# One more buffer for the rows of q and k, and three copies of v moved up on their queue

## The chip, the core and the metric

The kernel runs on one NeuronCore of a Trainium2 chip. The metric is the device time of one execution in microseconds (us), as the median over several runs. The profile is that of a single execution. Its engines are called PE (matrix multiply; PEld is the loading of its weights), DVE, ACT and POOL (element work), and SP, which here only issues DMAs and passes signals on. POOL issues DMAs of its own as well.

## What is computed

A layer normalisation of x (2048 tokens by 448), then two branches: attention with 16 heads of 28 over eight keys per query, two positions apart, and a feed-forward of width 1792. The two are multiplied and added to x.

```python
xn = _layernorm(x, axis=-1)
# A: q, k, v = xn @ wqkv; each query sees positions pos - 2*[0..7]
logits = einsum("bhsd,bhswd->bhsw", q, kg) * Dh ** -0.5     # masked below position 0
s = (softmax(logits) @ vg) @ wo
# B
g = silu(gelu(xn @ w1 + b1) @ w2 + b2)
return x + s * g
```

## The kernel before

**Tiles.** The tokens are put into 16 tiles of 128 (t = 0 to 15), even positions first, so that a dilation of two becomes neighbours. Four tiles make a chunk. The attention works on nine blocks of queries that do not coincide with the tiles: a block needs scores (L595, PE), exponentials (L605, ACT), a mask (L611, DVE or POOL), and the product with the values (L627, PE). The last step of all is the product with wo (L681), the gate and the sum.

**The order is written out.** Every piece of work is a task with a number, and the string ORDER (L17) lists all of them, with a letter for the engine that does each: P for PE, V for DVE, A for ACT, G for POOL, S for SP, D for the landing of a DMA. Each engine goes through its own tasks in this order and stops at the first one whose inputs are not there, with all behind it.

**The rows of q and k.** For a tile, PE makes q and k with tokens on partitions (L454, in `pair`, two outputs side by side in two banks). ACT and DVE copy each bank into a buffer of that tile in SBUF (`evac` of `qk_rows`, L456 to L464, the copies by the helper at L228 on ACT and L230 on DVE). Such a copy also frees its bank for PE. When both are done, SP issues one DMA that transposes the buffer into `qkT` (L276), where the scores read it. There are four such buffers, `qk_tok[t % 4]`, so the copies of tile t wait until the transpose of tile t - 4 has landed (`t_qk.get(t - len(qk_tok))`, L461). Their padding columns are zeroed once at the start, by one memset on DVE each (L255).

In the first two chunks the transposes are issued in the order t = 0, 2, 1, 3, with four transposes of `xn` between 2 and 1. The copies out of the banks for the second chunk stand in the order 6, 5, 4, 7 on ACT and on DVE. PE finishes the tiles of the second chunk in the order 6, 7, 5, 4. Behind the copies of tile 7, ACT has the first layer's activations (`ff1`, L516) and PE the matmuls that feed them (L512); these take the banks that the copies free, two for each pair of 512-column outputs.

**The copies of v.** v stays with tokens on partitions, in `v_tok[t]` (copied out of the banks by L228 and L230). A block's values must lie in windows of 64 rows that cross the tiles, so POOL issues DMAs that copy pieces of `v_tok` into one of six buffers `v` (`values` at L485, the DMA at L270). A copy whose piece belongs to a buffer that another copy has opened takes the same buffer. Tasks 407, 399, 403 and 405 copy rows of tile 8; 409, 411 and 415 copy rows of tile 9. Tasks 399, 403 and 405 fill the last rows of the buffers v2 and v3, which the fifth block's values read (the block in the middle, 56 queries wide). Tasks 409, 411 and 415 fill parts of v4 and v5 for the block after that. On POOL they stood as 407, 409, 411, 415, 399, 403, 405.

Every DMA of SP and of POOL raises one of eight semaphores in turn, and waits until the eighth DMA before it on its queue has landed.

Of the kernel before, what the change touches and what calls it, by code (L numbers as in the profile page):

```python
# [11 lines left out]
ACT = mybir.ActivationFunctionType  # L12
# [28 lines left out]
V744 P463 A464 A465 P468 S466 D467 G450 P451 V453 P442 G469 V751 P470 A471 V739 P435 S443 P444 V740 A446 A445 A566  # L41
G436 P437 A439 V753 V472 P754 V438 S440 D441 P868 P763 V452 V759 A766 V760 V869 P873 V870 V761 V567 V874 A768 A770
V762 A764 S447 D448 P578 P579 V580 A576 V577 V755 P781 A786 P373 A782 A788 V756 S871 D872 S861 D862 P583 S584 G374
P375 V376 G407 D408 P585 A784 A56 A377 P588 A581 S589 V757 G409 D410 V758 G411 D412 V767 V765 P593 P392 S594 A587
P590 P595 A586 G415 D416 V769 G399 D400 V771 V875 S393 A591 G403 D404 G473 P603 S876 D877 P394 S604 A597 P608 V395
A596 G405 D406 G413 D414 G417 D418 V789 G474 D475 P605 V787 A396 P772 G476 D477 G478 D479 G480 D481 A592 G482 D483
A606 V785 G484 D485 G486 D487 P598 V582 A607 S609 V773 V774 G488 D489 P613 V775 G490 D491 V783 S599 P600 G492 D493
V776 G494 D495 A602 A601 S614 P615 A616 P610 V777 V778 V779 V780 A612 P790 V795 P618 V791 A617 V796 A611 A57 P799
A800 V797 V798 G496 D497 P888 V889 P619 V620 P878 A804 V890 P883 A802 G498 D499 P817 S891 D892 V879 A818 V803 G500
# [69 lines left out]
def kernel(  # L119
# [13 lines left out]
    P = 128  # L133
    S, D, H, DH, F = A_x.shape[1], 448, 16, 28, 1792
# [16 lines left out]
    for v in range(9):  # L151
        n = NW - 1 if v == 4 else NW
        q = 4 * NW * v - 4 * (v > 4)
# [17 lines left out]
    def sb(name, shape, dt=BF16):  # L171
        return const.tile(shape, dt, name=name)
# [27 lines left out]
    def ring(name, n, shape, dt=BF16):  # L200
        return _Pool([sb(f"{name}{i}", shape, dt) for i in range(n)])
# [13 lines left out]
    p_g.bufs = p_g.bufs + late_g  # L215
    p_h = ring("h", 28, [P, CH])
    p_v = ring("v", 6, [P, H, 32])
    qk_tok = [sb(f"qk_tok{i}", [P, 2, H, 32]) for i in range(4)]
    p_b = _Pool([psum.tile([P, 512], F32, name=f"bank{i}") for i in range(8)])

    plan = _Plan()

    def buf(pool, owner, i=0):
        return pool.bufs[owner.slots[pool][i]]

    def copy(e, o, i):
        if e == "ACT":
            nc.scalar.copy(o, i)  # L228
        else:
            nc.vector.tensor_copy(o, i)  # L230


    def memset(eng, ap, v):
        def fn(_):
            getattr(nc, eng).memset(ap, v)
        return fn

    warm = p_h.bufs[-1]
    t_on = plan.add("DMA", lambda _: None, ())
# [12 lines left out]
                                base=0, pattern=[[-1, P]], channel_multiplier=1)  # L252
    t_ident = plan.add("POOL", mk_ident, [t_on])

    t_qz = [plan.add("DVE", memset("vector", q[:, :, :, DH:], 0.0), [t_on]) for q in qk_tok]  # L255
    t_vw = [plan.add("DVE", memset("vector", v[:, :, DH:], 1.0), [t_on]) for v in v_tok[:9]]
    t_row0 = plan.add("POOL", memset("gpsimd", row0[:], 0.0), [t_on])
    t_row0 = plan.add("POOL", memset("gpsimd", row0[:1, :], 1.0), [t_row0])
# [15 lines left out]
    def dma_T(dst, src, deps, give):  # L274
        def fn(_):
            nc.sync.dma_start_transpose(out=dst, in_=src())  # L276
        a = plan.add("SP", fn, deps)
        return plan.add("DMA", lambda _: None, [a], give=(give,) if give else ())
# [112 lines left out]
    def half_rows(half):  # L391
        return slice(64 * half, 64 * half + 64) if half < 2 else slice(0, P)
# [53 lines left out]
    t_row, t_qk = [[] for _ in range(NT)], {}  # L446

    def qk_rows(t, which):
        cs = slice(t * P, (t + 1) * P)

        def part(ps, kt, half, start, stop):
            r = half_rows(half)
            w = w_in[r, kt, which * D:(which + 1) * D] if kt < 3 else w_in3[r, 0, :]
            return nc.tensor.matmul(ps[:, :D], xnT[r, kt, cs], w, start=start, stop=stop)  # L454

        def evac(a, own, i):  # L456
            b = qk_tok[t % len(qk_tok)]

            def fn(k):
                copy(k.on, b[:, which, :, :DH], buf(p_b, own, i)[:, :D].rearrange("p (h c) -> p h c", h=H))  # L460
            t_row[t].append(plan.add(("ACT", "DVE"), fn, [a, t_qz[t % len(qk_tok)], t_qk.get(t - len(qk_tok))], give=((p_b, own, i),)))  # L461
            if len(t_row[t]) == 2:
                t_qk[t] = dma_T(qkT[:, :, :, cs].rearrange("p w g c -> p (w g) c"), lambda: b[:].rearrange("p w h c -> p (w h c)"),
                                t_row[t], None)  # L464
        return _Job(D, part, [t_xT[t]] + t_w[0] + t_w[1] + t_w[2], evac, (), t_w[3])
# [368 lines left out]
```

## Time and profile before

| | us |
|---|---|
| three runs | 156.47, 155.38, 156.09 |
| median | 156.09 |
| the profiled execution | 155.29 |
| its span, first to last instruction | 153.6 |
| the rest, outside the span | 1.7 |

| engine | busy us | share of the span |
|---|---|---|
| PE | 148.3 | 97% |
| DVE | 111.9 | 73% |
| ACT | 85.1 | 55% |
| POOL | 43.6 | 28% |

A row of the profile's groups or timeline names line, engine, operation and tile, with the output to the left of "<-". In a timeline row the first two numbers are start and length in us from the first instruction, "x" counts the instructions that were merged, and the bracket tells how long the engine sat idle before it and what ended that. Matmuls are pipelined and their ends modelled: the time that one takes from PE is the distance to the start of the next one, not its length.

### The profile page before, as it was taken

To read this page: it belongs to the slowest core of one execution; us is meant where nothing else is said; L and a number is where in the kernel's file an instruction comes from. 1 tells how busy PE (TensorE), PEld (TensorE's weight loads), DVE (VectorE), ACT (ScalarE), POOL (GpSimd) and SP (SyncE) were. 2 spreads that over 40 slices of the span, in tenths; PEclk is the share of its full clock that TensorE was granted. 3 is DMA by queue.
4 is the path that set the end of the run, shared out by engine and by line. 5 is a ranking of instruction groups with operands and counts; after the bars stand their busy time and mean duration, and the time that the engine had idled before them with its cause. 6 is when DMAs were issued, how large, how long until landed. Compare 5 with 4: busy or idle time off the path is not lost.

```text
span 153.6 us, 5265 instructions
## 1 busy us (share of the span) xinstructions
PE 148.3 (97%) x2200; PEld 80.9 (53%) x2200; DVE 111.9 (73%) x280; ACT 85.1 (55%) x158; POOL 43.6 (28%) x95
## 2 busy tenths in 40 slices
PE   6899999999999999999999999999999999999992
PEld 2444445578775555555554554455455444455561
DVE  4998541459262699969897997389859497797973
ACT  3474665368886350737043759739670859580320
POOL 7854865000359116020000004499500000000000
PEclk9999999999999999999999999999999999999999
DMA  5999998999987635079217370323300010010022
GB/s 149 326 276 324 126 187 168 226 343 257 165 112 150 111 73 103 4 147 131 63 34 137 74 132 19 98 71 86 81 30 4 4 60 30 4 47 17 0 89 65
DMA packets 33576, 17.36 MB, mean 113 GB/s; under 512 B 25203, under 2 KB 32387, under 8 KB 33552
## 3 DMA queue, kind: packets, MB, share of 16 engines
q1 hardware_dynamic: 31472, 14.03, 44.5%
q0 software_dynamic: 1936, 2.88, 7.9%
q8 instruction: 17, 0.28, 0.8%
q10 hardware_dynamic: 144, 0.11, 0.2%
q14 instruction: 7, 0.06, 0.1%
HBM read 7.06 MB, written 1.84 MB: 58 GB/s over the span
## 4 chain that ended last, share of the span: by engine, by line
PE 83%; DMA 5%; DVE 4%; POOL 3%; SPq 2%; issue 1%; ACT 1%; POOLq 0%; ACTq 0%
PE bank L546 28%; PE bank L512 22%; PE bank L454 10%; PE bank L681 8%; PE bank L477 6%; PE bank L627 4%; PE bank L595 4%; DMA qkT<-qk_tok 3%; POOL v L270 2%; DMA x_sb<-in_A_x_dram 2%; SPq L276 2%; DVE xn L363 1%; DVE st L329 1%; PE bank L378 1%; DVE xn L368 0%
## 5 line engine op out<-in xcount | busy, mean ns | idle before, releaser
L546 PE MATMUL bank<-w,h 128*128 128x448 bf16 (+2 forms) x238 | 45.1, 342 | 0.0
L512 PE MATMUL bank<-xnT,w 64*128 64x512 bf16 x392 | 44.7, 376 | 0.3 <-ACT qk_tok L228 0.3
L270 POOL DMA_DIRECT2D v<-v_tok x52 | 27.3, 532 | 48.4 <-DVE v_tok L230 27.1
L516 ACT ACTIVATE h<-bank,b 128x512 bf16<-128x512 f32 x56 | 34.2, 692 | 12.3 <-PE bank L512 12.2
L512 PEld LDWEIGHTS <-w 64*128 64x128 bf16 x392 | 23.1, 94 | 18.7 <-issue 1.0
L546 PEld LDWEIGHTS <-h 128*128 128x128 bf16 x238 | 22.1, 98 | 18.9
L605 ACT ACTIVATE E<-bank 128x456 bf16<-128x456 f32 (+1 forms) x36 | 17.2, 551 | 14.8 <-PE bank L595 14.8
L454 PE MATMUL bank<-w_in,xnT 64*128 64x448 bf16 (+1 forms) x212 | 24.0, 350 | 0.2 <-DVE xnT L230 0.2
L228 ACT CAST qk_tok<-bank 128x448 bf16<-128x448 f32 x20 | 9.9, 534 | 13.7 <-PE bank L454 9.8
L454 PEld LDWEIGHTS <-xnT 64*128 64x128 bf16 (+1 forms) x212 | 10.4, 94 | 10.1 <-issue 0.4
L561 DVE TENSOR_TENSOR y<-bank,b 128x448 f32<-128x448 f32 x15 | 9.2, 612 | 7.6 <-PE bank L546 7.6
L681 PE MATMUL bank<-wo,oT 128*128 128x448 bf16 (+2 forms) x68 | 14.3, 342 | 0.0
L637 DVE STREAM_TRANSPOSE dt<-bank 128x480 f32<-128x480 f32 (+1 forms) x18 | 11.8, 662 | 2.9 <-PE bank L627 1.7
L477 PE MATMUL bank<-w_in,xnT 64*128 64x448 bf16 (+1 forms) x106 | 13.8, 349 | 0.0
L230 DVE CAST qk_tok<-bank 128x448 bf16<-128x448 f32 x12 | 7.2, 620 | 8.7 <-PE bank L454 5.2
L646 DVE STREAM_TRANSPOSE dt<-rd 128x480 f32<-128x480 f32 (+1 forms) x18 | 12.0, 668 | 0.3
L329 DVE BATCH_NORM_STATS2 st<-x_sb 128x6 f32<-128x448 bf16 x16 | 9.7, 603 | 3.2 <-DMA x_sb<-in_A_x_dram 3.2
L651 DVE TENSOR_TENSOR oT<-bank,dt 128x456 bf16<-128x456 f32 (+1 forms) x18 | 11.1, 625 | 0.3
L611 DVE TENSOR_TENSOR E<-E,m_gen 128x456 bf16<-128x456 bf16 x28 | 10.0, 379 | 1.8 <-ACT E L605 1.8
L573 ACT ACTIVATE t<-y 128x448 f32<-128x448 f32 x12 | 6.9, 581 | 6.2 <-DVE y L561 6.2
L363 DVE TENSOR_SCALAR xn<-x_sb,mv,rstd 128x448 bf16<-128x448 bf16 x16 | 6.1, 394 | 4.7 <-POOL rstd L351 4.5
L230 DVE CAST v_tok<-bank 128x448 bf16<-128x448 f32 x9 | 5.6, 619 | 5.1 <-PE bank L477 5.1
(62 smaller groups left out, 120.6 us busy)
## 6 DMA issues: line engine op xcount, KB each, us to landing
out_dram<-o SPq DMA_DIRECT2D x15, 112.0 KB, 1.8
w<-in_B_w_dram SPq DMA_DIRECT2D x2, 784.0 KB, 7.4
w<-in_B_w_dram SPq DMA_DIRECT2D x2, 672.0 KB, 7.6
x_sb<-in_A_x_dram SPq DMA_DIRECT2D x3, 448.0 KB, 6.2
v<-v_tok POOLq DMA_DIRECT2D x20, 64.0 KB, 2.9
w_in<-in_A_wqkv_dram SPq DMA_DIRECT2D x3, 336.0 KB, 4.0
w<-in_B_w_dram SPq DMA_DIRECT2D x4, 112.0 KB, 7.1
wo<-in_A_wo_dram POOLq DMA_DIRECT2D x4, 98.0 KB, 3.8
```

The costliest lines, as they stand in the source:

```text
L230: nc.vector.tensor_copy(o, i)
L270: nc.gpsimd.dma_start(dst(k), src())
L329: nc.vector.bn_stats(out=buf(p_st, k)[:], in_=x_sb[:, t, :])
L454: return nc.tensor.matmul(ps[:, :D], xnT[r, kt, cs], w, start=start, stop=stop)
L477: return nc.tensor.matmul(ps[:, :D], xnT[r, kt, k0:k0 + P], w, start=start, stop=stop)
L512: return nc.tensor.matmul(ps[:], w1[r, kt, ms], xnT[r, kt, cs], start=start, stop=stop)
L516: nc.scalar.activation(buf(p_h, own, i)[:], buf(p_b, own, i)[:], ACT.Gelu_apprx_tanh, bias=b1[:, mt:mt + 1])
L546: nc.tensor.matmul(ps[:, :n], buf(*h_at[(c, mt)])[:, j * P:(j + 1) * P], w2[:, mt, cs], start=(mt == 0 and not biased), stop=(mt == NMT - 1))
L605: nc.scalar.activation(buf(p_E, k)[:, :n], buf(p_b, a, hl)[:, :n], ACT.Exp, scale=SCALE)
L637: nc.vector.transpose(buf(p_dt, k)[:, :32 * m], buf(p_b, po, i)[:, :32 * m])
L646: nc.vector.transpose(buf(p_dt, d)[:, :32 * m].rearrange("p (b c) -> p b c", c=32), buf(p_rd, r)[:, :m].unsqueeze(2).to_broadcast((P, m, 32)))
L681: nc.tensor.matmul(ps[:, :n], oT[:, kt, t * P:(t + 1) * P], wo[:, kt, cs], start=(kt == 0), stop=(kt == KT - 1))
```

## The change

A fifth buffer is added. Two of the five are the halves of one allocation, `qk_pair`, zeroed by one memset of double size, so that the count of tasks and their numbers stay as they were. A table `qk_at` says which tile has which buffer, and the copies of a tile wait for the transpose of the last earlier tile with the same buffer.

In ORDER the tasks G399, G403 and G405 (three copies of tile 8's v) stand in front of G409, G411 and G415 (three copies of tile 9's v). Nothing else in ORDER is moved, and no instruction is added or removed on any engine but that one memset is twice as wide.

```diff
-P375 V376 G407 D408 P585 A784 A56 A377 P588 A581 S589 V757 G409 D410 V758 G411 D412 V767 V765 P593 P392 S594 A587
-P590 P595 A586 G415 D416 V769 G399 D400 V771 V875 S393 A591 G403 D404 G473 P603 S876 D877 P394 S604 A597 P608 V395
-A596 G405 D406 G413 D414 G417 D418 V789 G474 D475 P605 V787 A396 P772 G476 D477 G478 D479 G480 D481 A592 G482 D483
+P375 V376 G407 D408 P585 A784 A56 A377 P588 A581 S589 V757 G399 G403 G405 G409 D410 V758 G411 D412 V767 V765 P593
+P392 S594 A587 P590 P595 A586 G415 D416 V769 D400 V771 V875 S393 A591 D404 G473 P603 S876 D877 P394 S604 A597 P608
+V395 A596 D406 G413 D414 G417 D418 V789 G474 D475 P605 V787 A396 P772 G476 D477 G478 D479 G480 D481 A592 G482 D483
 A606 V785 G484 D485 G486 D487 P598 V582 A607 S609 V773 V774 G488 D489 P613 V775 G490 D491 V783 S599 P600 G492 D493
...
-    qk_tok = [sb(f"qk_tok{i}", [P, 2, H, 32]) for i in range(4)]
+    qk_pair = sb("qk_pair", [P, 2, 2, H, 32])
+    qk_tok = [sb(f"qk_tok{i}", [P, 2, H, 32]) for i in range(3)] + [qk_pair[:, i] for i in range(2)]
+    qk_at = [0, 1, 2, 3, 4, 0, 2, 1, 3, 4, 0, 2, 1, 3, 4, 0]

-    t_qz = [plan.add("DVE", memset("vector", q[:, :, :, DH:], 0.0), [t_on]) for q in qk_tok]
+    t_qz = [plan.add("DVE", memset("vector", q[:, :, :, DH:], 0.0), [t_on]) for q in qk_tok[:3]]
+    t_qz += [plan.add("DVE", memset("vector", qk_pair[:, :, :, :, DH:], 0.0), [t_on])] * 2

-            b = qk_tok[t % len(qk_tok)]
+            b = qk_tok[qk_at[t]]
+            free = t_qk.get(max([u for u in range(t) if qk_at[u] == qk_at[t]], default=None))
...
-            t_row[t].append(plan.add(("ACT", "DVE"), fn, [a, t_qz[t % len(qk_tok)], t_qk.get(t - len(qk_tok))], give=((p_b, own, i),)))
+            t_row[t].append(plan.add(("ACT", "DVE"), fn, [a, t_qz[qk_at[t]], free], give=((p_b, own, i),)))
```

So the copies of the second chunk wait for other transposes than before:

| tile | waited for the transpose of | waits now for that of |
|---|---|---|
| 6 | 2 | 2 |
| 5 | 1 | 0 |
| 4 | 0 | none |
| 7 | 3 | 1 |

In the later chunks tile 8 waits for 3, 9 for 4, 10 for 5, 11 for 6, 12 for 7, 13 for 8, 14 for 9 and 15 for 10, where each waited for the tile four before it.

## The prediction

> **What bounds the kernel now.** I read the page's busy times and the row of slices first, then the chain of waits, then the timeline around the two places where the chain shows something other than steady matmuls.
>
> ```profile
> PE 148.3 (97%) x2200; PEld 80.9 (53%) x2200; DVE 111.9 (73%) x280; ACT 85.1 (55%) x158; POOL 43.6 (28%) x95
> PE   6899999999999999999999999999999999999992
> PEclk9999999999999999999999999999999999999999
> PE 83%; DMA 5%; DVE 4%; POOL 3%; SPq 2%; issue 1%; ACT 1%; POOLq 0%; ACTq 0%
> ```
>
> PE is the bound: busy in every slice from the third on, at full granted clock. But a matmul's end is modelled, so a short stop of PE hides in "busy". The chain shows where to look:
>
> ```profile
> 23.79 5.02 DMA qkT<-qk_tok
> 28.80 0.02 issue
> ...
> 28.88 0.54 ACT qk_tok L228
> 29.42 0.04 issue
> 29.46 12.38 PE bank L512 x112
> ...
> 100.27 0.96 PE bank L627 x64
> ...
> 105.01 0.61 PE bank L627 x64
> ...
> 149.62 0.70 PE bank L546 x14
> ```
>
> From 29.46 to the last row here all 72 pieces of the chain but the break at 67.24 (0.00 us of issue) are PE. So what PE gains before or at 100.27 is carried to the end, unless PE then meets something that does not come earlier with it. Before 29.46 the chain goes through a transpose of q and k rows (issued 23.79, landed 28.80) and the copy that waited for it. And one product with the values, at 100.27, is 0.96 us where its like at 105.01 is 0.61.
>
> **The first stall, 29 us.** The timeline, and a like place later on:
>
> ```profile
> 22.82 5.46 PE L454 MATMUL bank<-w_in,xnT 64*128 64x448 bf16 x56
> 25.10 0.62 DVE L230 CAST qk_tok<-bank 128x448 bf16<-128x448 f32 x1 [3.94 <-PE bank L454]
> 28.12 1.03 PE L512 MATMUL bank<-xnT,w 64*128 64x512 bf16 x8
> 28.88 0.97 ACT L228 CAST qk_tok<-bank 128x448 bf16<-128x448 f32 x2 [3.17 <-DMA qkT<-qk_tok]
> 28.93 1.71 DVE L230 CAST qk_tok<-bank 128x448 bf16<-128x448 f32 x3 [3.20 <-DMA qkT<-qk_tok]
> 30.06 0.53 ACT L228 CAST qk_tok<-bank 128x448 bf16<-128x448 f32 x1 [0.22 <-DMA qkT<-qk_tok]
> 91.31 1.03 PE L512 MATMUL bank<-xnT,w 64*128 64x512 bf16 x8
> 92.18 0.73 PE L477 MATMUL bank<-w_in,xnT 64*128 64x448 bf16 x6
> ```
>
> Eight matmuls of L512 take PE 92.18 - 91.31 = 0.87 us; after those that began at 28.12 the next should start at 28.99 and starts at 29.46. PE lost 0.47 us, waiting for the banks of tile 5, which ACT and DVE could copy out only when tile 1's transpose had landed at 28.80.
>
> What the change puts in its place: tile 5 waits for tile 0's transpose.
>
> ```profile
> L276 SPq DMA_TRANSPOSE qkT<-qk_tok x1: 1334/1334/1334, 11.3 to 11.3; - x1
> DMA to landing us min/median/max: 5.7/5.7/5.7
> ```
>
> That landed at 11.3 + 5.7 = 17.0, long before. So tile 5's copies start when PE has made its rows. PE's 56 matmuls of L454 run from 22.82 to 28.28; tile 5 is third to be finished, after 50 of them, about 22.82 + 50/56 × 5.46 = 27.70. Copies of 0.53 (ACT) and 0.62 (DVE) free the banks at 28.2 to 28.4, 0.6 us before PE wants them at 28.99. Tile 4 waits for no transpose: it is made at 28.28 and copied by 28.9. Tile 7 stands behind them on both engines and now waits for tile 1's landing, 28.80, about when they reach it; it is out by 29.5 where before it was out at 30.64 (the end of DVE's x3). PE takes tile 4's and 7's banks after 29.46 and did so without a wait, within the 12.38 us of the chain. It comes 0.47 earlier and they come 1.1 earlier, so no new stall follows: **gain 0.47**.
>
> On SP nothing moves: the transposes of tiles 5, 4 and 7 go out behind other DMAs, after 33.3, when even the old copies were done.
>
> ```profile
> 28.86 4.44 SPq L276 DMA_TRANSPOSE qkT<-qk_tok  x1
> ```
>
> In the third and fourth chunk each tile waits for a transpose that lies a chunk back or nearly, and PE had no wait for such a copy there in the chain: nothing. The memset is one instruction for two buffers:
>
> ```profile
> L235 DVE MEMSET qk_tok<- x4: 112/112/112, 1.8 to 2.1; 128x64 uint32 x4
> 0.79 2.58 DMA x_sb<-in_A_x_dram
> ```
>
> The wide one, which no row shows, takes between 0.11 and 0.22 us; four ended at 2.2, and DVE has then to wait for x until 0.79 + 2.58 = 3.37: nothing.
>
> **The second stall, 100 us.** Rows of POOL and around it:
>
> ```profile
> 93.89 0.52 POOL L270 DMA_DIRECT2D v<-v_tok  x1 [25.19 <-DVE v_tok L230]
> 94.77 3.10 POOL L270 DMA_DIRECT2D v<-v_tok  x6 [0.36 <-ACT v_tok L228]
> 99.82 9.83 POOL L270 DMA_DIRECT2D v<-v_tok  x19 [1.95 <-DVE v_tok L230]
> 100.20 1.03 PE L627 MATMUL bank<-E,v 64*32 64x56 bf16 x64
> L270 POOL DMA_DIRECT2D v<-v_tok x3: 512/517/527, 94.8 to 95.8; - x3
> DMA to landing us min/median/max: 1.8/1.8/1.9
> L270 POOL DMA_DIRECT2D v<-v_tok x3: 505/526/532, 96.3 to 97.3; - x3
> DMA to landing us min/median/max: 3.3/3.6/3.9
> ```
>
> The six at 94.77 are 409, 411, 415, then 399, 403, 405. The last three go out from 96.3 to 97.3 and land 3.9 to 3.3 us later, at 100.2 to 100.6, while the product that reads them begins at 100.20. That is its excess of 0.96 - 0.61 = **0.35**, the second gain. In the new order 399 follows 407 at once (same tile 8, already there): the three are issued at 94.4, 94.9 and 95.4. With the 1.9 us of their neighbours they land by 97.3, with the 3.9 of their own old time by 99.4; PE comes to them at 100.20 - 0.47 = 99.7. Either holds. The three that go back are issued at 96.0, 96.5 and 97.0, POOL is through by 97.5 (97.87 before), and stands idle until 99.82 in both orders, so nothing behind them on POOL moves. They are read by the product at 104.94, now 104.1: at 3.9 us they are there by 101.
>
> A rule of the Trainium skill, "DMA: Bandwidth & Descriptors", section "Anatomy of one DMA — SWDGE (gpsimd) path", speaks against this half: a DMA of POOL takes about 2.0 us and its bytes over 436 kB per us, an estimate of 2.15 us for a 64 KB copy. By it the three would have been there at 99.5, PE would have waited for something else, and the sum would be 0.47 alone. The landings of 3.3 to 3.9 us above differ from it.
>
> **The sum.** 0.47 + 0.35 = 0.82 us off. The profiled execution took 155.29 (span 153.6), so 154.47 for one like it. It was faster than all three timed runs (155.38 to 156.47); from their median, 156.09 - 0.82 = **155.3**.
>
> **The rivals.**
>
> *Only the first stall goes* (0.10). Copies land late for a reason that follows them, a busy spell of the DMA engines for instance, or what ends last at 100.20 is not they. For it: neighbours landed in 1.8 us and these in 3.3 to 3.9, unexplained. Against: the spell would have to come earlier too. 156.09 - 0.47 = 155.6.
>
> *Given back behind PE* (0.08). PE comes earlier and meets an engine that does not.
>
> ```profile
> 83.83 0.97 ACT L228 CAST qk_tok<-bank 128x448 bf16<-128x448 f32 x2 [0.76 <-PE bank L454]
> 85.17 0.53 ACT L228 CAST qk_tok<-bank 128x448 bf16<-128x448 f32 x1
> 85.77 0.70 PE L595 MATMUL bank<-qkT 32*64 32x56 bf16 x64
> ```
>
> Here the copy ends at 85.70 and PE starts at 85.77: if ACT stayed where it is, 0.40 of the 0.47 would be lost and 0.42 left, 155.7. Against it: ACT had waited 0.76 us for PE just before, so it moves with PE.
>
> *The stalls are longer in ordinary runs* (0.15). Both are waits for DMAs, whose times vary most, and the profiled run was the fastest seen by 0.09 to 1.18 us. If the 0.80 between it and the median lies in these two waits, the change removes it too: 154.5, at the edge of 1%.
>
> *The change does not free tile 5* (0.02): the two halves of one allocation might be taken for one buffer. Then tile 4 would wait for tile 3's transpose, landed at about 30.0 (ACT's copy at 30.06 waited for it). Tile 5 isn't in that buffer, and tile 4's banks are wanted only after two more groups of PE. Even then little is lost: between 155.3 and 155.6.
>
> *Slower* (0.03): the three copies that go back come too late for the product at 104.1. From issue at 97.0 that takes more than 7.1 us to start costing, and 7.9 us to eat both gains. A v copy's longest time in the trace is 6.6, a transpose's 8.1:
>
> ```profile
> DMA to landing us min/median/max: 1.6/2.8/6.6
> DMA to landing us min/median/max: 8.1/8.1/8.1
> ```
>
> At 8.1 PE would wait 1.0 us and the kernel end at 156.3. Both long times stand at 13 to 15 us, where the DMA engines are busy nearly throughout; at 97 us they are not.
>
> **How the numbers follow.** The forecast, both stalls gone and nothing given back, has 0.62. A per cent is 1.56 us, and the three runs lie 1.09 apart, so that is about what a measurement can tell from no change. The forecast, 0.82 us or 0.5%, and all rivals but one lie within it; half of the long-stall case and a chance of 0.07 for a lucky spread make 0.15 for faster, 0.04 stays for slower (a late copy that costs more than worked out, or something not seen), 0.81 for the same. The range for 8 in 10: down to 154.0, the 154.5 of the long stalls with part of the runs' spread; up to 156.4, where the given-back cases (155.7) end with the upper spread of 0.38, and the slower rival lies.
>
> **What would show it.** In the changed profile: the copies of tiles 5 and 4 on ACT start at about 27.7 and 28.3 with PE ending their wait, and only that of tile 7, if any, waits for a transpose; the eight matmuls at 28.1 are followed by the next at 29.0; the product with the values near 99.7 takes 0.61 like the others; POOL has four or more copies in one run from 93.4 on; the span is near 152.8. A stall of L512 near 30 would say that the wait has moved on to tile 7. A span of 153.6 with both stalls gone would say that PE lost the time again further back, and the distance of like PE rows in both traces would show at which row.

## The result, and the profile after

| | before | after |
|---|---|---|
| median of 22 runs each, us | 155.97 | 155.47 |
| lowest and highest | 155.15, 156.91 | 154.65, 155.96 |
| the profiled execution | 155.29 | 155.96 |
| its span | 153.6 | 154.2 |

The ratio of after to before is 0.9965, 95% interval 0.9949 to 0.9982: half a microsecond faster, with a gain between 0.3 and 0.8 us, well within the 1% that the forecast's likeliest case named. It had put the gain at 0.82 us. The profiled execution of after is the slowest of its 22 runs and that of before lies near the fastest of its own, so their spans are not to be set against each other; they are read place by place.

The page of after, its span, the busy time of PE and the engines of the chain; then the chain at the start:

```profile
span 154.2 us, 5265 instructions
PE 148.6 (96%) x2200; PEld 76.0 (49%) x2200; DVE 111.8 (72%) x280; ACT 85.2 (55%) x158; POOL 43.1 (28%) x95
PE 92%; DMA 4%; SPq 1%; DVE 0%; issue 0%; ACT 0%
```
```profile
2.68 6.62 DMA w_in<-in_A_wqkv_dram
9.29 0.04 issue
9.34 0.54 PE bank L457 x2
```

The chain is PE's as before, but it begins with the third load of `w_in`, landed at 9.29; in before the same load had landed at 7.90. The change does not touch it. PE starts its half-row matmuls (those with 64 rows) 1.34 us later than in before, and every place below is later by that much or by what is left of it.

Tile 5's banks. The timeline of after:

```profile
29.13 0.53 ACT L230 CAST qk_tok<-bank 128x448 bf16<-128x448 f32 x1 [2.07 <-PE bank L457]
29.15 0.62 DVE L232 CAST qk_tok<-bank 128x448 bf16<-128x448 f32 x1 [2.08 <-PE bank L457]
29.46 3.83 PE L516 MATMUL bank<-xnT,w 64*128 64x512 bf16 x34
29.69 0.53 ACT L230 CAST qk_pair<-bank 128x448 bf16<-128x448 f32 x1
29.73 0.62 DVE L232 CAST qk_pair<-bank 128x448 bf16<-128x448 f32 x1
30.12 0.54 ACT L230 CAST qk_tok<-bank 128x448 bf16<-128x448 f32 x1
30.27 0.61 DVE L232 CAST qk_tok<-bank 128x448 bf16<-128x448 f32 x1
```

The brackets of tile 5's copies name PE where they named a transpose. Tiles 4 (`qk_pair`) and 7 follow with no wait. L516 runs 34 matmuls in one row: no stop after the first eight.

The copies of v on POOL, and the product with the values; then the landings of the first four and of the last four of the seven copies:

```profile
94.66 3.60 POOL L273 DMA_DIRECT2D v<-v_tok  x7 [25.25 <-DVE v_tok L232]
100.97 0.68 PE L631 MATMUL bank<-E,v 64*32 64x56 bf16 x64
101.58 0.82 PE L516 MATMUL bank<-xnT,w 64*128 64x512 bf16 x6
```
```profile
L273 POOL DMA_DIRECT2D v<-v_tok x4: 510/524/539, 94.7 to 96.2; - x4
DMA to landing us min/median/max: 1.6/1.8/1.9
L273 POOL DMA_DIRECT2D v<-v_tok x4: 512/532/536, 96.2 to 97.7; - x4
DMA to landing us min/median/max: 1.9/3.8/4.0
```

Seven copies go out in one run. The product takes 101.58 - 100.97 = 0.61 us: the excess of 0.35 is gone. The copies of tile 8, second to fourth of the seven, land in at most 1.9 us. The long landings of 3.8 to 4.0 have passed to tile 9's copies (for the last of them the trace has none), which are there by about 101, four microseconds before the product at 105.35 that reads them.

So both waits went. What did not come out as worked out lies at the other end. The last store of the output, in before and in after, with the DMA queues of that stretch:

```profile
q1 hardware_dynamic: 288, 0.11, 16.7%
out_dram<-o SPq DMA_DIRECT2D x1, 28.0 KB, 1.4
```
```profile
q1 hardware_dynamic: 288, 0.11, 16.1%
q14 instruction: 1, 0.01, 0.7%
out_dram<-o SPq DMA_DIRECT2D x1, 28.0 KB, 1.7
```

The same store of 28 KB lands 1.4 us after its issue in before (first fence) and 1.7 in after, and in after a packet of the queue "instruction" stands in the stretch that was not there.

By PE's start times in both traces the account of these two executions is: 1.34 us behind from the start; 0.86 behind after the first stop is saved; 0.41 behind at the last matmul, with the second saved too (the remaining 0.10 is what follows a stop, treated below, less 0.03 that lies elsewhere); 0.65 behind at the end of the span, since the end came 0.24 later after the last matmul.

### The profile page after: what moved, and what is told of

Same layout as the page of the kernel before. It is cut to its first block, busy times and chain, and to the rows that moved or that the text cites. A ratio compares the mean times of both kernels' runs of the same rounds, so it can differ in the third digit from the quotient of the medians.

```text
span 154.2 us, 5265 instructions
## 1 busy us (share of the span) xinstructions
PE 148.6 (96%) x2200; PEld 76.0 (49%) x2200; DVE 111.8 (72%) x280; ACT 85.2 (55%) x158; POOL 43.1 (28%) x95
## 4 chain that ended last, share of the span: by engine, by line
PE 92%; DMA 4%; SPq 1%; DVE 0%; issue 0%; ACT 0%
PE bank L550 28%; PE bank L516 28%; PE bank L457 13%; PE bank L685 8%; PE bank L481 7%; DMA w_in<-in_A_wqkv_dram 4%; PE bank L599 4%; PE bank L631 4%; SPq L266 1%; PE bank L381 0%; DVE sg L691 0%; ACT w_in L572 0%; DVE o L699 0%; PE bank L548 0%; PE bank L772 0%
## 5 line engine op out<-in xcount | busy, mean ns | idle before, releaser
L516 PE MATMUL bank<-xnT,w 64*128 64x512 bf16 x392 | 44.3, 376 | 0.0
L516 PEld LDWEIGHTS <-w 64*128 64x128 bf16 x392 | 18.8, 94 | 22.4 <-issue 0.4
L232 DVE CAST qk_tok<-bank 128x448 bf16<-128x448 f32 x8 | 4.9, 622 | 7.6 <-PE bank L457 7.3
L230 ACT CAST qk_tok<-bank 128x448 bf16<-128x448 f32 x12 | 6.0, 534 | 4.5 <-PE bank L457 3.6
```

The lines of the kernel that those rows point to most:

```text
L516: return nc.tensor.matmul(ps[:], w1[r, kt, ms], xnT[r, kt, cs], start=start, stop=stop)
```

## The experiments

Thirteen profiles stand in one table. "First stop" is the time that PE lost after the eight half-row matmuls of the second chunk, "second" the excess of the values product over 0.61, "tail" the time from the start of PE's last matmul to the end of the span, all from the start times of the records (so 0.48 for the 0.47 of the prediction). "Transpose" is the time from issue to landing of tile 1's transpose. "Late fetch" is the start of the last 8 KB packet of an instruction queue, and ACT's count that of its instructions in the compiled program, the waits among them.

| kernel | first stop | transpose | second | tail | late fetch | ACT's count |
|---|---|---|---|---|---|---|
| before | 0.48 | 5.02 | 0.35 | 3.28 | 148.7 | 197 |
| before_again | 0.32 | 4.86 | 0.00 | 3.28 | 149.0 | 197 |
| before_third | 1.23 | 5.77 | 0.59 | 3.28 | 150.4 | 197 |
| before_fourth | 0.00 | 3.75 | 0.12 | 3.28 | 148.8 | 197 |
| order_only | 0.15 | 4.71 | 0.00 | 3.26 | 148.8 | 197 |
| buffers_only | 0.00 | 5.27 | 0.12 | 3.50 | 151.2 | 196 |
| after | 0.00 | 4.98 | 0.00 | 3.52 | 152.1 | 196 |
| after_again | 0.00 | 3.75 | 0.00 | 3.77 | 152.1 | 196 |
| after_third | 0.00 | 5.28 | 0.00 | 3.74 | 151.3 | 196 |
| five_apart | 0.00 | 4.98 | 0.00 | 3.59 | 151.7 | 196 |
| tile5_waits_for_3 | 1.72 | 5.00 | 0.00 | 3.63 | 153.3 | 196 |
| one_more_on_act | 0.00 | 5.10 | 0.00 | 3.28 | 147.9 | 197 |
| one_fewer_on_act | 0.63 | 5.16 | 0.00 | 3.37 | 154.4 | 195 |

(A fourteenth, one_more_again, has 0.00, 5.00, 0.00, 3.27, 147.7 and 197.)

### The two halves of the change, each alone

buffers_only has the fifth buffer and its table with the old order:

```diff
-    qk_tok = [sb(f"qk_tok{i}", [P, 2, H, 32]) for i in range(4)]
+    qk_pair = sb("qk_pair", [P, 2, 2, H, 32])
+    qk_tok = [sb(f"qk_tok{i}", [P, 2, H, 32]) for i in range(3)] + [qk_pair[:, i] for i in range(2)]
+    qk_at = [0, 1, 2, 3, 4, 0, 2, 1, 3, 4, 0, 2, 1, 3, 4, 0]
```

> The fifth buffer and its table alone, the order as before. Forecast's theory: only the first stall goes: the group of eight L512 matmuls near 28 to 30 us is followed by the next after 0.87 us (excess 0.00, before 0.47), the values' product near 100 us keeps an excess near 0.35 over 0.61. Time 0.47 us below before, ratio 0.997. Rival A, the stalls are smaller in ordinary runs than in the profiled one: the excess goes all the same, but the time falls by 0.2 to 0.35 only. Rival B, the change costs something at the start (the weights of q, k, v land later with the new buffers): the first matmul that waits for them starts 1 us or more later than in profiles of before, and the time falls by less than 0.3.

order_only has the new order with the four old buffers (the three copies are taken out where they stood, as in the diff of the change):

```diff
-V757 G409 D410 V758 G411 D412 V767 V765
+V757 G399 G403 G405 G409 D410 V758 G411 D412 V767 V765
```

> The three copies of v moved up alone, four buffers as before. Forecast's theory: the first stall stays near 0.47, the values' product near 100 us takes 0.61 (excess 0.00), time 0.35 us below before, ratio 0.998. Rival A: the product takes 0.61, but the time falls by less than 0.2, since in ordinary runs the copies came nearer to being in time. Rival B says the same as the forecast here, as no buffer is new.

after_again and before_again are the two kernels once more, on the same chip.

> The changed kernel once more. Forecast's theory: both excesses 0.00 again, 0.82 us below before; the 22 runs say 0.50. Rival A: excesses 0.00, some 0.5 us below before. Rival B: the weights land late again (first profile: the third landing at 9.3 us, against 7.9 before).

> The kernel before, for a second profile. Forecast's theory: stalls of 0.47 and 0.35 us again, within 0.1. Rival A: at least one of them 0.15 us or more smaller, their sum near 0.5. Rival B: stalls as in the first profile, and the weights' third landing near 7.9 us again.

Against 155.91 for the kernel before, buffers_only took 155.61 (ratio 0.9975, 0.995 to 1.0001), order_only 155.41 (0.9966, 0.9937 to 0.9995), the whole change 155.26 (0.9952, 0.9926 to 0.9979); before_again, a single run, 155.56. The intervals overlap, so the shares of the halves can't be told from times. Nor did the two stops of before_again come out as expected: 0.32 and 0.00 us, where 0.47 and 0.35 stood in the forecast. The traces tell which wait belongs to which half. buffers_only, timeline:

```profile
28.35 4.91 PE L516 MATMUL bank<-xnT,w 64*128 64x512 bf16 x44
29.31 0.53 ACT L230 CAST qk_tok<-bank 128x448 bf16<-128x448 f32 x1 [0.20 <-DMA qkT<-qk_tok]
99.87 0.80 PE L631 MATMUL bank<-E,v 64*32 64x56 bf16 x64
100.60 1.68 PE L516 MATMUL bank<-xnT,w 64*128 64x512 bf16 x14
```

The first stop is gone; tile 7's copy did wait 0.20 us for tile 1's transpose, as worked out, and PE was not held up. The product still takes 100.60 - 99.87 = 0.73. order_only, timeline:

```profile
29.31 0.97 ACT L228 CAST qk_tok<-bank 128x448 bf16<-128x448 f32 x2 [2.84 <-DMA qkT<-qk_tok]
94.36 3.60 POOL L270 DMA_DIRECT2D v<-v_tok  x7 [25.25 <-DVE v_tok L230]
100.68 0.68 PE L627 MATMUL bank<-E,v 64*32 64x56 bf16 x64
```

Here the copies still wait for the transpose (the stop was 0.15 us this time) and the product's excess is gone.

An excess of zero proves little by itself, since two of the six profiles with the old order have none either. What the product waits for can be read inside it. From the chain of before_third, a profile described further down:

```profile
97.75 4.18 DMA v<-v_tok
101.92 0.04 issue
101.97 0.93 PE bank L627 x63
```

There the three copies of tile 8 land at 101.92, 102.09 and 102.25, and PE, stopped within the product, goes on at 101.97, 102.13 and 102.30. In before they land at 100.27, 100.43 and 100.59, and PE goes on at 100.31, 100.47 and 100.63. In before_fourth and buffers_only only the last of them lands after the product has begun, at 100.66 and 100.02, and PE goes on at 100.70 and 100.07. In the two profiles of the old order without an excess no landing on record comes after the start of the product. So each half takes away its own wait, and only that.

### A wait of known size in the same place

tile5_waits_for_3 is the changed kernel with another table, in which tile 5 takes the buffer of tile 3, whose transpose lands latest:

```diff
-    qk_at = [0, 1, 2, 3, 4, 0, 2, 1, 3, 4, 0, 2, 1, 3, 4, 0]
+    qk_at = [0, 1, 2, 3, 4, 3, 2, 1, 0, 4, 3, 2, 1, 0, 4, 3]
```

> The changed kernel with another table: tile 5 has the buffer of tile 3 instead of that of tile 0, so its copies wait for a later transpose than before the change. Five profiles so far: that transpose is issued 2.92 us before the eight L512 matmuls begin and lands 4.6 to 5.2 us after its issue. Theory (the first stall is the landing of the awaited transpose, whose length varies from run to run, against PE, which comes a fixed time after the issue): after the eight matmuls PE stops for landing time - 3.13, 1.5 to 2.1 us; the product near 100 us stays at 0.61; time 1.5 to 2.2 us over the changed kernel's, 0.9 to 1.6 over before. Rival (the wait costs little, the gain comes from elsewhere, such as the layout): within 0.4 us of the changed kernel.

Its timeline:

```profile
28.79 1.03 PE L516 MATMUL bank<-xnT,w 64*128 64x512 bf16 x8
30.79 0.97 ACT L230 CAST qk_pair<-bank 128x448 bf16<-128x448 f32 x2 [4.41 <-DMA qkT<-qk_pair]
31.37 2.00 PE L516 MATMUL bank<-xnT,w 64*128 64x512 bf16 x16 [1.56 <-ACT qk_pair L230]
```

The transpose of tile 3 took 4.86 us here; less the 3.13 named beforehand that makes 1.73. PE stands still for 31.37 - 28.79 - 0.865 = 1.72 us, and the median is 157.44 against 156.28 (ratio 1.0086, 1.0054 to 1.0118). Against the changed kernel, some 0.5 us under before, the price is about 1.7 us: within what the times can tell, a wait put in at this place is paid in full at the end.

### Five separate buffers, and the kernel before twice more

five_apart gives each of the five buffers its own allocation, with the memset task of the pair made into two memsets:

```diff
-    qk_pair = sb("qk_pair", [P, 2, 2, H, 32])
-    qk_tok = [sb(f"qk_tok{i}", [P, 2, H, 32]) for i in range(3)] + [qk_pair[:, i] for i in range(2)]
+    qk_tok = [sb(f"qk_tok{i}", [P, 2, H, 32]) for i in range(5)]
...
+    def zero_two(_):
+        for q in qk_tok[3:]:
+            nc.vector.memset(q[:, :, :, DH:], 0.0)
+    t_qz += [plan.add("DVE", zero_two, [t_on])] * 2
```

> The changed kernel with five separate buffers and two narrow memsets in one task. Theory: the halves of one allocation are told apart already, so nothing changes: no stop after the eight L512 matmuls, product near 100 us at 0.61. Rival (the shared allocation has a part in where the time went): a copy of tile 3, 4, 8, 9, 13 or 14 starts earlier against PE, or the stretches of PE between the two places are more than 0.1 us shorter than in the changed kernel.

> The kernel before, third profile. Theory (both stalls vary with the landing of single DMAs): first stall = landing time of tile 1's transpose - 4.54 us, within 0.05, wherever it lies between 0 and 0.7; the second anything from 0 to 0.36. Rival (the first profile was odd in one thing only): the same 0.32 and 0.00 as in the second profile.

> The kernel before, fourth profile, as the third: first stall = landing time of tile 1's transpose - 4.54 us; the mean of both stalls over the four profiles together 0.45 to 0.65 us, which is the gain of the changed kernel's median, and not 0.82.

five_apart (155.61, one run) shows at tile 5 what after shows:

```profile
28.80 1.54 ACT L229 CAST qk_tok<-bank 128x448 bf16<-128x448 f32 x3 [2.07 <-PE bank L460]
29.14 4.05 PE L519 MATMUL bank<-xnT,w 64*128 64x512 bf16 x36
```

So the halves of one allocation are told apart as well as two allocations. The two profiles of the kernel before lie 1.6 us apart, three times the whole gain of the change; before_third (156.95) and then before_fourth (155.36):

```profile
28.75 1.03 PE L512 MATMUL bank<-xnT,w 64*128 64x512 bf16 x8
30.26 1.60 ACT L228 CAST qk_tok<-bank 128x448 bf16<-128x448 f32 x3 [3.92 <-DMA qkT<-qk_tok]
30.84 2.45 PE L512 MATMUL bank<-xnT,w 64*128 64x512 bf16 x20 [1.06 <-ACT qk_tok L228]
```
```profile
28.60 1.10 ACT L228 CAST qk_tok<-bank 128x448 bf16<-128x448 f32 x2 [2.07 <-PE bank L454]
28.93 4.26 PE L512 MATMUL bank<-xnT,w 64*128 64x512 bf16 x38
```

In the first the transpose of tile 1 took 5.77 us and PE lost 1.23; in the second 3.75 us and PE lost nothing. In every profile with the old buffers the first stop is the transpose's time less 4.54, or nothing where that is negative: 5.02 gives 0.48, 4.86 gives 0.32, 5.16 gives 0.62 where 0.63 was measured, and the largest difference is 0.02 (order_only). The stop is the overhang of one DMA over a fixed lead, and it varies with that one DMA.

After a stop the stretch from the start of the eight matmuls to that of the scores is longer by the stop and some 0.13 us more (16.34 us without a stop, 16.95 with the 0.48, 17.70 with the 1.23). The mean cost over the six profiles with old buffers, the 16.34 taken off each, is 0.58 us. The mean excess of the values product in the six with the old order is 0.20. Together 0.77 us of PE's time, close to the 0.82 that was forecast. The times gave 0.5. What had been expected for before_fourth, that the mean of both stops over four profiles would be 0.45 to 0.65 us and so explain the times, failed: 0.51 and 0.26 make 0.77. The tail's column has the rest.

### One instruction on ScalarE

With 196 instructions on ACT the tail is 3.50 to 3.77 us in six profiles of six; with 197 it is 3.26 to 3.28 in seven of seven. The fifth buffer changes which copies need a separate waiting instruction: ACT has one fewer, DVE one more. DVE's count was no explanation: it is 337 in after, 338 in five_apart and 336, as in before, in tile5_waits_for_3, all three with the long tail. one_more_on_act puts an instruction back on ACT where it has nothing to do:

```diff
-    plan.add("ACT", lambda _: nc.scalar.activation(sd[:, :1], eps_t[:], ACT.Sqrt), [t_eps])
+    def first_sqrt(_):
+        for _ in range(2):
+            nc.scalar.activation(sd[:, :1], eps_t[:], ACT.Sqrt)
+    plan.add("ACT", first_sqrt, [t_eps])
```

> The changed kernel with the first activation of ScalarE (a 128x1 square root at 2.5 us, 0.20 us long) made twice; ScalarE has nothing to do for 1.79 us behind it. In the four profiles of the kernel before, and in that of the changed order with the old buffers, the end of the span comes 3.26 to 3.28 us after the start of the last matmul; in the five profiles with the fifth buffer 3.50 to 3.77 us. There the last store lands 1.67 to 1.92 us after its issue in place of 1.43, and an 8 KB instruction fetch that stood at 148.7 us comes at 151.2 to 153.3 us, between that store's issue and its landing. ScalarE has one waiting instruction fewer with the fifth buffer (196 in place of 197). Theory, the missing instruction moved the fetch to the end of the program: with one instruction more on ScalarE the fetch is back near 148.7, the last store lands 1.43 after its issue, the tail is 3.28, both stops of PE stay away, and the median is 0.2 to 0.4 us under the changed kernel's in the same rounds. Rival, the tail belongs to something else in the fifth buffer (its place in SBUF, VectorE's count): tail 3.50 to 3.77 and a median like the changed kernel's. Rival, the fetch moves but the tail is not its doing: fetch near 148.7 and a tail of 3.5 or more.

> The changed kernel once more, as the measure for the run with one more instruction on ScalarE on the same chip. Theory: no stop behind the eight half-row matmuls of tiles 4 and 5, values product 0.61, tail 3.50 to 3.77 us, ratio to the kernel before 0.994 to 0.998. If the tail is a matter of chance from run to run and not of the instruction stream, it may come out at 3.28.

The timeline of one_more_on_act has the second root, with 1.52 us of idle time left behind it; then the DMA view around its last store, and that of after_third:

```profile
2.50 0.44 ACT L315 ACTIVATE sd<-eps_t 128x1 f32<-128x1 f32 x2
4.46 0.29 ACT L347 ACTIVATE sd<-mv,eps_t 128x1 f32<-128x1 f32 x1 [1.52 <-DVE mv L339]
```
```profile
q1 hardware_dynamic: 288, 0.11, 17.5%
out_dram<-o SPq DMA_DIRECT2D x1, 28.0 KB, 1.4
```
```profile
q1 hardware_dynamic: 288, 0.11, 15.0%
q14 instruction: 1, 0.01, 0.7%
out_dram<-o SPq DMA_DIRECT2D x1, 28.0 KB, 1.9
```

With one instruction more the fetch is back at 147.9, the store lands after 1.4 us and the tail is 3.28. Both stops are away in both kernels. The waiting instruction that ACT lost is still missing here (32 of them in both, 33 in before), so it is not the absence of that wait as such which makes the tail. The median is 154.90 against 155.21 for the changed kernel in the same rounds (12 runs each), ratios to before 0.9955 (0.9933 to 0.9976) and 0.9964 (0.9941 to 0.9988). The 0.31 between them is near what the tails say (0.35 on average), but the intervals overlap; the trace, not the time, carries the verdict.

one_fewer_on_act goes the other way, from the kernel before:

```diff
-    plan.add("ACT", lambda _: nc.scalar.activation(sd[:, :1], eps_t[:], ACT.Sqrt), [t_eps])
+    plan.add("ACT", lambda _: None, [t_eps])
```

> The kernel before, without the first activation of ScalarE (a 128x1 square root of a constant at 2.5 us, whose result nothing reads); its table load stays where it was. With it one wait goes too, so ScalarE has 195 instructions in place of 197, and q and k buffers and order are untouched. Theory, ScalarE's count decides where the last 8 KB instruction fetch falls: the fetch comes near 151 to 153 us, behind the issue of the last store, that store lands 1.67 to 1.92 us after its issue, the tail is 3.5 to 3.8 us in place of 3.28, and the median is 0.1 to 0.5 us above the kernel before. Rival, the long tail belongs to the fifth buffer's place in SBUF: tail 3.28 and a median like the kernel before. If two instructions fewer carry the crossing past the end of the program altogether, there is no such fetch and the tail is 3.28 with one fetch fewer in the list.

> The changed kernel with one activation more on ScalarE, a second time. Theory: fetch near 148, last store landing 1.43 after its issue, tail 3.26 to 3.28, no stop of PE at tile 5 nor in the values product, ratio to the kernel before 0.993 to 0.997, and a median 0.2 to 0.4 us under that of the changed kernel's rounds. If the 0.3 us of the first such run were chance, the ratio is that of the changed kernel, 0.996 to 0.998, with the tail at 3.28 all the same.

The main expectation for one_fewer_on_act failed. Its median is 155.94 against 155.88 (1.0011, 0.9986 to 1.0037), and its last store lands 1.44 us after its issue, as in before.

What happened is near the last of the cases written down for it: with two instructions fewer the fetch did not vanish but went past the end, to 154.42, 0.31 us behind the end of the span and long after the store had landed. So three counts give three places: 197 puts the packet at about 148 to 150, ahead of the last store; 196 between the last store's issue and its landing; 195, in the one profile there is, behind everything. Only the middle one has a late store. The tail with 195 is 3.37 all the same: the 0.09 over 3.28 lie nearly all behind the landing, and why is open. The packet times beside the last store, from the DMA records:

```
                    store issued  landed   last 8 KB fetch
before (197)            151.20    152.63       148.69
after (196)             151.61    153.28       152.14
one_more_on_act (197)   150.45    151.88       147.90
one_fewer_on_act (195)  151.65    153.09       154.42
```

one_more_again took 154.66 against 155.88 (0.9931, 0.9907 to 0.9955), with a tail of 3.27. Over all its 18 runs the version with one instruction more has a median of 154.89, the changed kernel over all its 46 runs, most of them in other rounds, 155.34. It has the lowest median of those tried, though the intervals of its ratios and of the changed kernel's overlap.

## Why the prediction was right, and where its sum was not

**The bound.** Right. PE carries the chain in every profile, and a stop put in ahead of 100 us is paid at the end (tile5_waits_for_3). From the values product to the last matmul PE takes 49.13 us, within 0.01, in all fourteen profiles.

**The first stall.** Right in mechanism: it goes with the buffers alone, tile 5's copies wait for PE, tile 7's wait moves to tile 1's landing (0.20 us in buffers_only) and costs nothing. As a size the 0.47 was one draw: 0.00 to 1.23 in six profiles with the old buffers. That its own mean there is 0.47 as well is luck; with the 0.13 us that follow a stop, which the prediction had left out, the mean cost is 0.58.

**The memset.** Hidden, and within its bounds of 0.11 and 0.22; the row of after:

```profile
2.07 0.17 DVE L237 MEMSET qk_pair<- 128x128 uint32 x1
```

**The second stall.** Right in mechanism: it goes with the order alone, PE goes on where the old order's copies land, and the copies put back are there by about 101 as worked out. Its size, 0.35, was above the mean of 0.20 (0.00 to 0.59). The rule of the Trainium skill ("DMA: Bandwidth & Descriptors", section "Anatomy of one DMA — SWDGE (gpsimd) path") that would have left this half at nothing, an estimate of 2.15 us for a 64 KB copy, does not hold for all of these copies: those of one row of seven landed in 1.6 to 4.0 us in after, and it depended on when they were issued, not on their size.

**The sum.** What failed in it is the sentence that what PE gains "is carried to the end, unless PE then meets something that does not come earlier with it". PE met nothing. But its last matmul is not the end, and behind it the kernel with the fifth buffer takes 0.22 to 0.49 us longer, 0.35 on average over six profiles. The prediction had no term for that. It went by the section on the change, which says that no instruction is added or removed; that holds for the tasks, not for the separate waiting instructions that the compiled program has beside them, of which ACT lost one. 0.77 on PE less 0.35 behind it leaves 0.42, within the 0.3 to 0.8 that was measured. The forecast of 155.3 came within 0.2 of the 155.47, in part by luck: the gain was 0.3 short of the 0.82, and the median of before over 22 runs came 0.12 below the 156.09 that the forecast started from.

**The rivals.** "Given back behind PE" was right in kind, and had 0.08: some 0.3 us are given back. It named a copy at 85.7 us as the place, and there nothing was lost. "Only the first stall goes" falls, though its 155.6 lay near. "The stalls are longer in ordinary runs" falls as a rule: the mean of both is 0.77. They do cost 1.36 + 0.59 us in a long execution such as before_third, and the changed kernel has neither; its highest time of 22 runs is 0.95 under the highest of before. That the change doesn't free tile 5 falls with after and five_apart. The slower one, late copies, did not come: 101 against 105.35.

**The start.** after's profile began 1.34 us later on PE than before's. Nothing says that this is the fifth buffer's doing: the half-row matmuls begin at 10.02 to 10.83 us in six profiles with the old buffers and at 10.04 to 11.36 in eight with the new, with a mean of 10.61 for both.

## What to carry to other kernels

Where an engine that sets the end waits for a single DMA, read the wait as the DMA's time less the lead that it has, and take several executions before a size is given to it: here one stop was anything from 0 to 1.23 us. Follow a gain past the last instruction of the bounding engine, to the landing of the last store. Where a tail grows by some tenths for no visible reason, look in the DMA view for an instruction packet behind the last store's issue, and compare the instruction counts, waits included.

## What the runs showed of the hardware

Instructions are fetched while the program runs, over the same DMA engines as the data. The queues of before's page:

```profile
q8 instruction: 17, 0.28, 0.8%
q14 instruction: 7, 0.06, 0.1%
```

The Trainium skill, "Trainium Architecture — The Big Picture", section "The software stack", has the instruction streams moved into each engine's own memory when the program is loaded. It speaks there of the load alone; these rows show 24 packets more within the span.

One 8 KB packet of 0.31 to 0.49 us, between the issue of a 28 KB store and its landing, goes with a landing 0.24 to 0.49 us later. How is open. The store's last data packet ends 1.09 us after its issue without the fetch and 1.09 to 1.20 with it; the landing follows 0.34 to 0.35 us behind that without, 0.53 to 0.73 with the fetch. So it is mostly the notice of the end that comes late, and little of it the data. Which engine's fetch it is, no record says; it moves with ACT's count and not with DVE's.

A stop of PE costs more than its length: 0.13 us or so in addition over the next 16 us, at 0.15 as at 1.23. Why was not tried.

The v copies issued between 96.3 and 97.7 us land late, at about 100 to 101, in before and after alike and whichever copies they are: the same copy of 1 KB took 3.59 us in before, where it was the sixth of the seven, and 1.64 in after, where it was the third. They follow one 16 KB instruction packet, which starts at 97.38 in before and lasts 1.55 us. In fourteen profiles the first late copy lands 0.99 to 1.39 us behind the end of that packet; in the six with the old order, where it is always the same copy, 1.30 to 1.39 us, while its time from issue to landing runs from 3.47 to 4.18. In before fifteen 4 KB packets of a late copy run at 97.59 to 97.90 and one more alone at 99.59, 0.66 us behind the end of the instruction packet; in before_third and in after such a lone one comes 0.66 and 0.67 behind it. So it looks as if one share of each late copy stands behind the fetch on one of the DMA engines. But the records name no engine, in before_third the fetch starts only after the fifteen, and no run moved this fetch: the cause is likely and not shown.
